# A segment's stored keys and queries fetched as one group of four loads, two of them into unused partitions of the value tiles

## The chip, the cores and the metric

The kernel runs on one core of a Trainium2 chip. The metric is the device time of one execution in microseconds, the median of three runs. The engines are named as in the profile: PE is TensorE (PEld its weight load), DVE is VectorE, ACT is ScalarE, POOL is GpSimd and SP is SyncE; L1130 is line 1130 of the kernel.

## The reference, cut to what matters

Four layers, A, B, A, B, each added to its input, on 2048 tokens of 640 features. Only the A layers matter here:

```python
for s in range(n_seg):                      # 64 segments of 32 tokens
    h = concat([mem, xs])                   # 8 memory rows + 32 tokens = 40
    q, k, v = h @ Wq, h @ Wk, h @ Wv        # 32 heads of 192
    p = softmax(where(mask, q @ k.T * scale, -1e9))
    o = (p @ v) @ Wo
    mem = o[:8]                             # the next segment needs these
    outs.append(o[8:])
```

The memory rows of one segment come out of the segment before, so the 64 segments of a layer form a chain.

## The kernel before, in words

**Stored tokens.** Of a segment's 32 tokens, 24 pass through the chain together with the 8 memory rows; the keys, queries and values of the last 8 tokens don't depend on the memory and are worked out ahead of the chain for all segments (`A_pre`) and kept in DRAM: `kqb_d[round, partition, segment, 192]` for keys and queries, `vb_d` for values. The output rows of these tokens ("tails") take a way of their own.

**Rounds.** The 32 heads are worked through in four rounds of eight heads, numbered here 0 to 3 in the order in which a segment takes them (even segments take the heads forwards, odd ones backwards: `rounds(s)`). For each round the chain projects queries, keys and values of the 32 live rows (`project`, L1154), ACT moves them out of PSUM (L1169), DVE transposes them into the tile `QK` (L1174), POOL copies the round's stored keys and queries next to them, in columns 64 to 79 of each block of 80 (`extra_kq`, L1130), PE forms the scores (`scores`, L1191), ACT the exponentials (L1273), and PE multiplies by the values (`attend`, L1204; L1217 for the tail rows). The values stand in one of two tiles `Vs[n % 2]`: partitions 0 to 63 come from the projection (`v_rows`, L1181 and L1183), partitions 64 to 79 from `vb_d` by a DMA (`extra_v`, L1134); matmuls read partitions 0 to 79, and partitions 80 to 127 are unused. At a segment's end the output projection (L1263) is finished, and DVE writes the new memory rows (L1453, L1455), on which the next segment's first query matmul waits.

**Order.** The scheduling in the chain is manual: each engine runs its instructions in the order in which the program lists them, and the queues of POOL and SP too, so that an instruction behind a waiting one waits as well. POOL issues nearly all the small DMAs. Its order in a segment before the change:

- Rounds 0 to 2, each: copies for the next round (`next_kq`, L1391, behind the scores of this round, since the copies overwrite what these read), a load of values (`tails_after`, L1405; in round 2 it comes behind the next scores, L1428), and one load of stored keys and queries, for three rounds later (`fetch_kq`, L1406), into one of two tiles `kqb`. In round 2 a store of tail rows (L1256) as well.
- Round 3: the value load for the next segment's round 0 (L1428), the copies for that round (L1429), the value load for its round 1 (L1435), one load of keys and queries (L1436), the rows of the segment after next (`load_rows`, L1101), and the tail loads (`load_tails`, L247), if there are any; then the stores of the finished rows (L1119, L1256).

**Tail loads.** The values of stored tokens for the later segments are worked out in the chain itself, a piece a segment. Their tokens are fetched once in eight segments: at the end of a segment `load_tails(s + 1)` (L1449) issues two loads, and in the next segment `turn_tails` (L1362) has DVE transpose them (L250), behind the value eviction of round 0 and ahead of the transposes of round 1's keys and queries. This happens for segments 7, 15, 23, 31, 39 and 47 of each chain, 24 loads in all.

**Start of a chain.** Two loads of stored keys and queries and two value loads are issued, the copies for the first round made, and a third load issued (L1323 on), while SP streams weights.

Of the kernel before, what the change touches and what calls it, by code (L numbers as in the profile page):

```python
# [8 lines left out]
P = 128  # L9
# [113 lines left out]
class Kernel:  # L123
# [934 lines left out]
    def A_chain(self, xn_dram, at_dram, li, load_slot, piece, late_wo, load_both, wo, low):  # L1058
        nc, tc, KC, NSEG = self.nc, self.tc, self.KC, self.NSEG
        scale = float(self.Dh) ** -0.5  # L1060
        NR = 4
        with tc.tile_pool(name=f"A{li}_ch", reuse_waits="tile", bufs=1) as sp, \
# [55 lines left out]
            def store_rows(s):  # L1118
                nc.gpsimd.dma_start(out=self.rows_d[32 * s:32 * s + 32, :].rearrange("t (q f) -> q t f", q=4), in_=orow)  # L1119

            def load_kqb(s, r):
                kqb = sp.tile([P, 192], BF16, name="kqb", tag="kqb", bufs=2)
                nc.gpsimd.dma_start(out=kqb[:], in_=self.kqb_d[r, :, s, :])  # L1123
                return kqb

            def extra_kq(kqb):
                for b in range(2):
                    h = slice(64 * b, 64 * b + 64)
                    o = QK[h].rearrange("p m (x c) j -> p (m x) c j", x=2)[:, :, b:b + 3, 64:80]
                    nc.gpsimd.tensor_copy(out=o, in_=kqb[h, :].rearrange("p (x c q) -> p x c q", c=3, q=16))  # L1130

            def extra_v(s, n):
                r = rounds(s)[n]
# [170 lines left out]
                    nc.scalar.activation(out=self.two_heads(vt), in_=ps[:, 0:384].rearrange("p (e f) -> p e f", e=2), func=ACT.Copy)  # L1304
                    self.store_values(nc.sync, vt, k, *unit)

            turns = [(s, r) for s in range(NSEG) for r in rounds(s)]

            def next_kq(s, n):

                at = NR * s + n + 1
                if at < len(turns):
                    extra_kq(kqs.pop(0))

            def fetch_kq(s, n):

                if s == 1:
                    self.copy_tails((2 * n, 2 * n + 1))
                at = NR * s + n + 3
                if at < len(turns):  # L1320
                    kqs.append(load_kqb(*turns[at]))

            kqs = [load_kqb(0, r) for r in rounds(0)[0:2]]  # L1323
            late_wo(0)
            extra_v(0, 0)
            extra_v(0, 1)
            extra_kq(kqs.pop(0))
            kqs.append(load_kqb(0, rounds(0)[2]))
            load_rows(1)
            for s in range(NSEG):  # L1330
                W = pop.tile([P, 512], F32, name="ps_w", tag="w")
                order = rounds(s)
                L = NR - 1

                def q_or_k(m, n, halves=False):
                    ps = psk if m == "K" else psq
                    project(hT, ps, m, n, s, range(KC))
                    return to_rows(ps, m, halves)

                def v_banks():  # L1340
                    return pop.tile([P, 512], F32, name="ps_v", tag="v")

                def tails_after(n):
                    if n + 2 < NR:
                        extra_v(s, n + 2)
                    elif s + 1 < NSEG:
                        extra_v(s + 1, n + 2 - NR)

                if s > 0:
                    keep_rows(W_done)  # L1350
                    rows = tail_rows(rct, spare_rows())
                    otb = turn_tail(rows)
                    store_rows(s - 1)
                    store_tail(otb, s - 1, rounds(s - 1)[L])
                turn_rows(q_or_k("Q", 0))
                turn_rows(q_or_k("K", 0))
                if s == 0:
                    late_wo(3, range(OWN // 2))
                pv = v_banks()
                project(hT, pv, "V", 0, s, range(KC))  # L1360
                v_rows(pv, 0, "sv")
                turn_tails(s)  # L1362
                OTs = []

                def turn(n, osc):
                    if n in (0, 2):
                        rows = (raw_of["K"][:, 0:384] if n else ots).rearrange("p (c j) -> p c j", j=64)
                        OTs.append([rows[:, 3 * G:3 * G + 3, :] for G in range(2)])
                        nc.vector.transpose(out=rows, in_=osc.rearrange("p (c j) -> p c j", j=64))
                        return  # L1370
                    if n == L:
                        OTs.append([KT[:, 3 * G:3 * G + 3, 0:64] for G in range(2)])
                    else:
                        OTs.append([vt[:, VH * G:VH * G + 192].rearrange("p (c j) -> p c j", j=64) for G in range(2)])
                    parts = osc if n == L else [osc[:, 192 * G:192 * G + 192] for G in range(2)]
                    for v, part in list(zip(OTs[n], parts))[::-1 if n == L else 1]:
                        nc.vector.transpose(out=v, in_=part.rearrange("p (c j) -> p c j", j=64))  # L1377

                outs = [(j, i) for j in range(L) for i in range(0, 12 if j else OWN, 2)]

                def output_steps(n):
                    for j, i in outs[0:n]:
                        wo_round(W, order[j], OTs[j], False, False, range(i, i + 2))
                    del outs[0:n]

                for n in range(L):
                    raw = q_or_k("Q", n + 1)
                    if n == 2:
                        otb = turn_tail(otr)
                    E = weigh()  # L1390
                    next_kq(s, n)  # L1391
                    turn_rows(raw)
                    if n == 1:
                        step = wo_round(W, order[0], OTs[0], True, False, range(OWN, 12))
                        if s == NSEG - 1:
                            load_both(order[L], True)
                            self.kept_tails = []
                            self.release(step, 12)
                            tails = self.kept_tails
                        else:  # L1400
                            load_both(order[L], False)
                    raw = q_or_k("K", n + 1, n + 1 == L)
                    O = attend(E, n)
                    if n != 2:
                        tails_after(n)  # L1405
                    fetch_kq(s, n)  # L1406
                    if n == 2:
                        store_tail(otb, s, order[1])
                    rc = weigh_rows(O)
                    if n == 1:  # L1410
                        rct = weigh_tail()
                    turn_rows(raw)
                    if n == L - 1:
                        output_steps(STEPS[0])
                    pv = v_banks()
                    project(hT, pv, "V", n + 1, s, range(KC))
                    if s == 0 and n == 1:
                        late_wo(1)
                        late_wo(2)
                    osc = raw_of["Q"][:, 0:384]  # L1420
                    for G in range(2):
                        scaled(osc[:, 192 * G:192 * G + 192], O, rc, G, "s")
                    turn(n, osc)
                    v_rows(pv, n + 1, "sv")
                    if n == 1:
                        otr = tail_rows(rct, raw_of["K"][:, 0:192])
                E = weigh(E)
                tails_after(2)  # L1428
                next_kq(s, L)  # L1429
                output_steps(STEPS[1])  # L1430
                if s + 1 < NSEG:
                    hT = new_hT()
                    hx_transpose(hT)
                O = attend(E, L)
                tails_after(L)  # L1435
                fetch_kq(s, L)  # L1436
                rc = weigh_rows(O)
                oscs = [raw_of["Q"][:, 192 * G:192 * G + 192] for G in range(2)]
                for G in (1, 0):
                    scaled(oscs[G], O, rc, G, "s")  # L1440
                keep_values()
                turn(L, oscs)
                output_steps(len(outs))
                if s == NSEG - 1:
                    self.spread_tails(0, tails[0], low, "vv")
                if s + 2 < NSEG:
                    load_rows(s + 2)
                wo_round(W, order[L], OTs[L], False, True, (*range(6, 12), *range(6)))
                load_tails(s + 1)  # L1449
                next_values(s)  # L1450
                if s + 1 < NSEG:
                    wt = raws[:, 0:640].bitcast(F32).rearrange("p (a b t) -> p a b t", a=2, b=KC)
                    nc.vector.transpose(out=wt, in_=W[:, 0:320].rearrange("p (a j b) -> p a b j", a=2, b=KC))  # L1453
                    for a in range(2):
                        nc.vector.tensor_tensor(out=hT[64 * a:64 * a + 64, :, 0:8], in0=wt[0:64, a, :, 0:8],  # L1455
                                                in1=wt[64:P, a, :, 0:8], op=ALU.add)
                rct = weigh_tail()
                W_done = W
# [92 lines left out]
```

## Time and profile before

| | |
|---|---|
| median of three runs | 3176.66 us (3176.52 to 3177.76) |
| profiled execution | 3169.9 us, span 3168.0 us |
| granted TensorE clock, mean | 0.992 |
| POOL copies of stored keys and queries, L1130 | 1024 of 341 ns |
| their loads, L1123 | 512 of 48 KB, 571 ns of POOL each, landing 4.3 us after issue (median) |
| value loads, L1134 | 512 of 24.2 KB, 504 ns, landing after 3.8 us |
| row loads, L1101, and row stores, L1119 | 126 and 128, 713 ns each |
| tail loads, L247 | 24 of 40 KB, 686 ns (median), landing after 5.2 us |

Durations of instructions and the sums in the text come from the one profiled execution, whose own time stands beside its span; the runs that give the median aren't profiled. A line of a wait list says which engine and line sat idle, until what was done, for how many us in total, how many times, and how long at most. A line of the instructions in order of time gives the start and the length in us, engine, line, operation, output and input with shapes, how many instructions are merged in it, and in brackets the idle time ahead of it with what ended it.

### The profile page before, as it was taken

Reading aid. Unit: us, or ns where it says so; the run is one execution under the profiler, and the core shown is the slowest. Engines: PE = TensorE matmul, PEld = TensorE weight load, DVE = VectorE, ACT = ScalarE, POOL = GpSimd, SP = SyncE. Lnnn points to the kernel's source line nnn. Section 1 sums busy time; section 2 is a strip of 40 time slices with the busy share of each in tenths; the row PEclk is TensorE's granted clock in tenths of the full one; section 3 lists DMA queues with packets and bytes.
Section 4 is the critical chain, followed back from the end, with each engine's and each line's share of the span. In section 5 each row is a group of like instructions: output and inputs, shape, how many; then the busy total and the mean of one; then the engine's idle time right before and its main releaser. Section 6 shows DMA issues by size and latency. Waiting matters only on the chain.

```text
span 3168.0 us, 141538 instructions
## 1 busy us (share of the span) xinstructions
PE 2993.8 (95%) x59586; PEld 1920.6 (61%) x59586; DVE 2184.4 (69%) x5426; ACT 1906.3 (60%) x4536; POOL 1392.8 (44%) x2872
## 2 busy tenths in 40 slices
PE   8789999999999999899999999999999999998999
PEld 7656666666666665555377566666666666665553
DVE  5467777777777777656644677777777777776565
ACT  3356666666666666646433566666666666666453
POOL 3255555555555555430122555555555555554300
PEclk9999999999999999999999999999999999999999
DMA  9977777877877877840268777777877777778300
GB/s 377 340 263 257 261 248 251 265 257 250 272 252 251 267 256 246 288 166 1 103 246 320 257 255 246 263 264 245 264 259 249 255 261 255 246 259 287 130 1 34
DMA packets 338873, 749.67 MB, mean 237 GB/s; under 512 B 68874, under 2 KB 115330, under 8 KB 335166
## 3 DMA queue, kind: packets, MB, share of 16 engines
q1 hardware_dynamic: 267998, 636.89, 58.3%
q0 software_dynamic: 69376, 100.10, 10.9%
q8 instruction: 469, 7.68, 1.0%
q10 hardware_dynamic: 864, 3.64, 0.3%
q14 instruction: 166, 1.36, 0.1%
HBM read 670.77 MB, written 78.01 MB: 236 GB/s over the span
## 4 chain that ended last, share of the span: by engine, by line
PE 76%; DVE 8%; DMA 6%; issue 5%; ACT 3%; POOL 2%; ACTq 0%; DVEq 0%; SPq 0%; POOLq 0%
PE ps_qk_k L1154 13%; PE ps_qk_q L1154 13%; PE ps_v L1154 12%; PE ps_w L1263 11%; PE ps_s L1191 6%; PE ps_pre L985 4%; PE ps_o L1204 3%; PE kv L1506 2%; DVE raws L1453 2%; ACT raws L1234 2%; DVE hT L1455 2%; PE ps_pq L517 2%; PE ps_t L1217 1%; PE ps_wo L466 1%; DVE QK L1377 1%
## 5 line engine op out<-in xcount | busy, mean ns | idle before, releaser
L1154 PEld LDWEIGHTS <-hT 128*32 128x32 bf16 x30720 | 787.1, 96 | 461.0 <-DVE hT L1455 78.7
L1174 DVE STREAM_TRANSPOSE QK<-raws 128x512 bf16<-128x512 bf16 (+1 forms) x1152 | 730.0, 642 | 219.3 <-ACT raws L1169 163.7
L1130 POOL COPY QK<-kqb 64x192 bf16<-64x192 bf16 x1024 | 349.5, 341 | 486.6 <-PE ps_s L1191 254.1
L1154 PE MATMUL ps_qk_q<-arena,hT 128*32 128x384 bf16 x10240 | 511.3, 327 | 41.4 <-DVE hT L1455 25.6
L1154 PE MATMUL ps_qk_k<-arena,hT 128*32 128x384 bf16 x10240 | 510.1, 328 | 3.0 <-ACT E L1273 1.4
L1169 ACT ACTIVATE raws<-ps_qk_k 128x512 bf16<-128x512 f32 (+1 forms) x640 | 313.5, 510 | 254.0 <-PE ps_qk_k L1154 243.5
L1234 ACT ACTIVATE raws<-ps_o,under 128x192 bf16<-128x192 f32 x1024 | 373.8, 420 | 121.9 <-DVE under L1228 102.5
L1154 PE MATMUL ps_v<-arena,hT 128*32 128x384 bf16 x8192 | 428.4, 326 | 4.0 <-issue 3.0
L1169 ACT ACTIVATE raws<-ps_qk_q 128x512 bf16<-128x512 f32 x512 | 305.7, 597 | 166.6 <-PE ps_qk_q L1154 153.1
L1134 POOL DMA_DIRECT2D Vp<-vb x512 | 257.9, 504 | 316.6 <-PE ps_t L1217 210.7
L1123 POOL DMA_DIRECT2D kqb<-kqb x512 | 292.4, 571 | 69.7 <-POOL QK L1130 59.4
L1191 PEld LDWEIGHTS <-QK 128*80 128x80 bf16 x4096 | 196.0, 121 | 184.9 <-issue 153.8
L1183 DVE CAST Vp<-ps_v 64x384 bf16<-64x384 f32 x512 | 286.3, 559 | 24.5 <-ACT Vp L1181 8.7
L1263 PE MATMUL ps_w<-arena,under 128*32 128x320 bf16 x6144 | 280.6, 300 | 9.5 <-DMA arena<-wo_rows 4.1
L1191 PE MATMUL ps_s<-QK 128*80 128x80 bf16 x4096 | 253.4, 209 | 21.8 <-POOL QK L1130 13.6
L1181 ACT ACTIVATE Vp<-ps_v 64x384 bf16<-64x384 f32 x512 | 246.4, 481 | 35.1 <-PE ps_v L1154 33.6
L1273 ACT ACTIVATE E<-ps_s 80x320 bf16<-80x320 f32 x512 | 217.7, 425 | 42.8 <-PE ps_t L1217 28.6
L985 PEld LDWEIGHTS <-arena 128*128 128x128 bf16 x1920 | 187.9, 98 | 31.0 <-issue 4.7
L1119 POOL DMA_DIRECT2D attn<-under x128 | 91.3, 713 | 262.0 <-DVE under L1115 223.5
L1112 ACT ACTIVATE raws<-ps_w 64x160 f32<-64x160 f32 x256 | 76.6, 299 | 201.1 <-DVE raws L1453 199.6
L1204 PE MATMUL ps_o<-Vp,E 80*32 80x193 bf16 x4096 | 180.3, 248 | 10.2 <-issue 5.7
L1263 PEld LDWEIGHTS <-under 128*32 128x32 bf16 x6144 | 147.2, 96 | 41.6 <-issue 9.8
(167 smaller groups left out, 4360.5 us busy)
## 6 DMA issues: line engine op xcount, KB each, us to landing
arena<-wo_rows SPq DMA_DIRECT2D x560, 320.0 KB, 4.8
arena<-in_A_Wq_dram SPq DMA_DIRECT2D x427, 384.0 KB, 4.5
arena<-in_A_Wk_dram SPq DMA_DIRECT2D x298, 384.0 KB, 5.6
arena<-in_A_Wv_dram SPq DMA_DIRECT2D x290, 384.0 KB, 5.9
kqb<-kqb POOLq DMA_DIRECT2D x512, 48.0 KB, 4.3
kqb<-arena POOLq DMA_DIRECT2D x14, 1536.0 KB, 9.7
Vp<-vb POOLq DMA_DIRECT2D x512, 24.2 KB, 3.8
otb<-otb POOLq DMA_DIRECT2D x256, 48.0 KB, 4.0
```

Source lines behind the costliest of these rows:

```text
L985: nc.tensor.matmul(ps[:, T * i:T * i + T], lhsT=w[b][:, P * c:P * c + P], rhs=xBT[:, b, :], start=(b == 0), stop=(b == KC - 1))
L1123: nc.gpsimd.dma_start(out=kqb[:], in_=self.kqb_d[r, :, s, :])
L1130: nc.gpsimd.tensor_copy(out=o, in_=kqb[h, :].rearrange("p (x c q) -> p x c q", c=3, q=16))
L1134: nc.gpsimd.dma_start(out=Vs[n % 2][64:80, :], in_=self.vb_d[s // 8, r].rearrange("g (t s) x f -> s (g t) (x f)", s=8)[s % 8])
L1154: last = nc.tensor.matmul(o, lhsT=hT[:, b, :], rhs=rhs, start=(i == 0), stop=(i == KC - 1), tile_position=(0, 32 * g), skip_group_check=True)
L1169: nc.scalar.activation(out=raw[:, c], in_=ps[:, c], func=ACT.Copy)
L1174: nc.vector.transpose(out=o, in_=i)
L1183: nc.vector.tensor_copy(out=o, in_=i)
L1191: nc.tensor.matmul(S[0:80, c0:c0 + 80], lhsT=KT[:, 4 * x + c, :], rhs=QT[:, 4 * x + c, :], start=(c % 2 == 0), stop=(c % 2 == 1), skip_gro ...
L1204: nc.tensor.matmul(O[G][32 * h:32 * h + 32, VH * G:VH * G + 193], lhsT=E[0:80, 80 * h + 32 * G:80 * h + 32 * G + 32], rhs=V[0:80, VH * h:V ...
L1234: nc.scalar.activation(out=out, in_=i, func=ACT.Copy, scale=rc[G])
L1263: step = nc.tensor.matmul(W[q:q + 32, 0:320], lhsT=OT[i // 6][:, i % 6 // 2, 32 * (i % 2):32 * (i % 2) + 32], rhs=rhs, start=(first and i ...
```

## The change

`load_kqb` takes the position of the round in its segment. The loads for positions 0 and 1 still go to a `kqb` tile of 128 partitions. Those for positions 2 and 3 go to partitions 96 to 127 of the value tiles, four pieces of 32 partitions side by side, 192 columns each; `extra_kq` then makes four copies of 32 partitions instead of two of 64, from partitions 96 to 127 to each quarter of `QK`. All four loads that a segment's copies will need next (its rounds 1, 2, 3 and the following segment's round 0) are issued as one group, in round 3 of the segment in front, behind the copies made there and ahead of the value load, the row load and the tail loads. The loads in rounds 0 to 2 and the one behind the value load of round 3 are gone. At the start of a chain one load is issued, and the group for the first segment behind the first copies.

```diff
-            def load_kqb(s, r):
+            def load_kqb(s, n):
+                rows = self.kqb_d[rounds(s)[n], :, s, :]
+                if n > 1:
+                    kqb = Vs[n % 2][96:P, 0:768].rearrange("p (g q) -> p g q", g=4)
+                    nc.gpsimd.dma_start(out=kqb, in_=rows.rearrange("(g p) q -> p g q", g=4))
+                    return [kqb[:, g, :] for g in range(4)]
                 kqb = sp.tile([P, 192], BF16, name="kqb", tag="kqb", bufs=2)
-                nc.gpsimd.dma_start(out=kqb[:], in_=self.kqb_d[r, :, s, :])
-                return kqb
+                nc.gpsimd.dma_start(out=kqb[:], in_=rows)
+                return [kqb[0:64, :], kqb[64:P, :]]
 
             def extra_kq(kqb):
-                for b in range(2):
-                    h = slice(64 * b, 64 * b + 64)
-                    o = QK[h].rearrange("p m (x c) j -> p (m x) c j", x=2)[:, :, b:b + 3, 64:80]
-                    nc.gpsimd.tensor_copy(out=o, in_=kqb[h, :].rearrange("p (x c q) -> p x c q", c=3, q=16))
+                step = P // len(kqb)
+                for i, rows in enumerate(kqb):
+                    o = QK[step * i:step * i + step].rearrange("p m (x c) j -> p (m x) c j", x=2)
+                    b = step * i // 64
+                    nc.gpsimd.tensor_copy(out=o[:, :, b:b + 3, 64:80], in_=rows.rearrange("p (x c q) -> p x c q", c=3, q=16))
...
-            def next_kq(s, n):
-
-                at = NR * s + n + 1
-                if at < len(turns):
+            def next_kq():
+                if kqs:
                     extra_kq(kqs.pop(0))
 
-            def fetch_kq(s, n):
-
-                if s == 1:
-                    self.copy_tails((2 * n, 2 * n + 1))
-                at = NR * s + n + 3
-                if at < len(turns):
-                    kqs.append(load_kqb(*turns[at]))
-
-            kqs = [load_kqb(0, r) for r in rounds(0)[0:2]]
+            def fetch_kqs(s):
+                kqs.extend(load_kqb(s, n) for n in range(1, NR))
+                if s + 1 < NSEG:
+                    kqs.append(load_kqb(s + 1, 0))
+
+            kqs = [load_kqb(0, 0)]
             late_wo(0)
             extra_v(0, 0)
             extra_v(0, 1)
-            extra_kq(kqs.pop(0))
-            kqs.append(load_kqb(0, rounds(0)[2]))
+            next_kq()
+            fetch_kqs(0)
             load_rows(1)
...
                     O = attend(E, n)
                     if n != 2:
                         tails_after(n)
-                    fetch_kq(s, n)
+                    if s == 1:
+                        self.copy_tails((2 * n, 2 * n + 1))
...
                 E = weigh(E)
                 tails_after(2)
-                next_kq(s, L)
+                next_kq()
+                if s + 1 < NSEG:
+                    fetch_kqs(s + 1)
                 output_steps(STEPS[1])
...
                 O = attend(E, L)
                 tails_after(L)
-                fetch_kq(s, L)
+                if s == 1:
+                    self.copy_tails((2 * L, 2 * L + 1))
```

More of the change, by code (lines that the diff above doesn't have):

```diff
@@ L1305, in keep_values @@
                     self.store_values(nc.sync, vt, k, *unit)
-            turns = [(s, r) for s in range(NSEG) for r in rounds(s)]
-            def next_kq(s, n):
-                at = NR * s + n + 1
-                if at < len(turns):
+            def next_kq():
+                if kqs:
                     extra_kq(kqs.pop(0))
-            def fetch_kq(s, n):
-                if s == 1:
-                    self.copy_tails((2 * n, 2 * n + 1))
-                at = NR * s + n + 3
-                if at < len(turns):
-                    kqs.append(load_kqb(*turns[at]))
-            kqs = [load_kqb(0, r) for r in rounds(0)[0:2]]
+            def fetch_kqs(s):
[3 more added lines that the diff above has]
+            kqs = [load_kqb(0, 0)]
             late_wo(0)
@@ L1428, in A_chain @@
                 tails_after(2)
-                next_kq(s, L)
+                next_kq()
+                if s + 1 < NSEG:
+                    fetch_kqs(s + 1)
                 output_steps(STEPS[1])
```

1 line of the change is left out of this document (removed).

## The prediction, made before the changed kernel was run

> **What bounds the kernel now.** I read the page's first part, then the waits, then a usual segment instruction by instruction, then the segments that start late.
>
> ```profile
> PE 2993.8 (95%) x59586; PEld 1920.6 (61%) x59586; DVE 2184.4 (69%) x5426; ACT 1906.3 (60%) x4536; POOL 1392.8 (44%) x2872
> ```
>
> TensorE is busy for 95% of the span, and nearly all of it lies in the 128 segments (64 in each of the two chains), which run one behind the other. Segments take 17.93 us at least and 18.3 us in the median (from one first query matmul to the next). So what counts is only what makes TensorE wait. GpSimd, where the change is made, is busy for 44%; 642 of its 1393 us are the copies (L1130, 349.5) and load issues (L1123, 292.4) that the change touches. The waits (who waited for whom: us in total, times, longest) tell whether it holds TensorE:
>
> ```profile
> PEld L1191 <- issue: 153.8, 470, 1.3
> POOL QK L1130 <- DMA kqb<-kqb: 129.4, 83, 5.0
> ...
> PEld L1191 <- POOL QK L1130: 30.1, 44, 13.8
> ```
>
> In the second line the copies at L1130 sat 129.4 us on stored keys and queries that had not landed. The third is what of it reached the scores: 30.1 us. But 13.8 of that is one wait, at the start of the first chain, and the first line says that a score's weight load has 153.8/470 = 0.33 us of idle time ahead of it anyhow. The other 43 waits are 16.3 us, less 43 x 0.33 = 14.1: **about 2 us** are truly lost. A usual segment shows why (start, us, engine, line):
>
> ```profile
> 615.62 0.50 PE L1191 MATMUL ps_s<-QK 128*80 128x80 bf16 x8
> ...
> 616.59 0.74 POOL L1130 COPY QK<-kqb 64x192 bf16<-64x192 bf16 x2 [1.15 <-DMA kqb<-kqb]
> ...
> 618.23 0.50 PE L1191 MATMUL ps_s<-QK 128*80 128x80 bf16 x8
> ```
>
> The copies for the last round waited for their DMA, ended at 617.33, and the scores that read them came 0.9 us later.
>
> **A place where GpSimd's order does reach TensorE.** In a usual segment the second round's scores start 3.205 us after the first's. Apart from the first segment of each chain, 10 segments are 0.2 to 1.7 us late with them, all of them segments in which turn_tails moves a freshly loaded set of tail rows (12 do: 7, 15, ... 47 of each chain; the other two are on time). One of them:
>
> ```profile
> 286.64 0.49 POOL L1134 DMA_DIRECT2D Vp<-vb  x1
> ...
> 287.19 0.60 POOL L1123 DMA_DIRECT2D kqb<-kqb  x1
> ...
> 287.79 0.71 POOL L1101 DMA_DIRECT2D xr<-xn  x1
> ...
> 288.49 1.36 POOL L247 DMA_DIRECT2D under<-tails  x2
> ...
> 292.74 0.47 PE L1191 MATMUL ps_s<-QK 128*80 128x80 bf16 x8
> ...
> 293.58 0.38 DVE L250 STREAM_TRANSPOSE tT<-under 128x160 bf16<-128x160 bf16 x1 [0.39 <-DMA under<-tails]
> ...
> 294.56 0.37 DVE L250 STREAM_TRANSPOSE tT<-under 128x160 bf16<-128x160 bf16 x1 [0.61 <-DMA under<-tails]
> ...
> 294.85 0.67 DVE L1174 STREAM_TRANSPOSE QK<-raws 128x512 bf16<-128x512 bf16 x1
> ...
> 295.64 0.69 DVE L1174 STREAM_TRANSPOSE QK<-raws 128x512 bf16<-128x512 bf16 x1
> ...
> 296.48 0.47 PE L1191 MATMUL ps_s<-QK 128*80 128x80 bf16 x8 [0.46 <-DVE QK L1174]
> ```
>
> The two tail loads are the last of four kinds of DMA that GpSimd issues back to back; VectorE waits for them at L250, and its next two transposes are the keys and queries of round 1. Measured from the first round's scores, the twelve second L250 transposes end at 2.19, 1.89, 1.20, 1.98, 2.51, 2.58 (first chain) and 3.15, 2.07, 3.40, 1.93, 1.39, 2.66 us, and the next scores start at 3.73, 3.44, 3.21, 3.53, 4.06, 4.13, 4.69, 3.61, 4.94, 3.47, 3.20, 4.21: always 1.54 us behind, once that is past 3.205. The wait isn't made up later: the three latest have segments of 20.40, 19.74 and 19.98 us.
>
> **The change, part by part.** Against the profiled execution's own 3169.9 us (span 3168.0).
>
> 1. *The group of four loads.* It is issued behind the copies of the last round, in front of the Vp load, the xr load and the tail loads; the single kqb load that stood there goes. The two loads into a kqb tile cost 0.571 us of issue each (L1123's mean). The two into 32 partitions by four pieces have no row: from below the same 0.571, from above the 0.713 of L1101 and L1119, which also split rows in four; I take 0.713, the nearer form. The group is 2 x 0.571 + 2 x 0.713 = 2.57 us, less 0.57: the Vp load of the next segment's second round, xr and the tails start **2.0 us later** (1.7 at the low end, and then 20 in place of this part's 23.3). The Vp load starts 11 us before its use and lands in 3.8, xr a segment ahead; the row stores behind them wait for VectorE 1.6 to 2.0 us already, and nothing waits for them within the segment; the next copies have 1.5 us of idle time ahead of them. All this costs nothing, and 0.5 us a segment if that idle time were gone. The tail loads have no cover: with the same time to landing, ten of the twelve segments get 2.0 us more, and the two that are on time use up 0.46 and 0.27 of slack: 20.0 + 1.54 + 1.73 = **+23.3 us**.
>
> 2. *Their landing.* They land 4.0 to 6.1 us after issue (median 5.2). The DMA engines are 0.20 busy in the last 2.4 us of a segment and 0.99 from 4 us on, as the windows show (the fields behind POOL's: granted clock, DMA share, GB/s), so a later issue meets more weights:
>
> ```profile
> 604.70:608.70 4.00, 3.97 (x92) 2.55 (x96) 3.16 (x7) 2.74 (x6) 1.37 (x3) 1.00 0.76 211
> 608.70:612.70 4.00, 4.00 (x108) 2.74 (x104) 3.21 (x6) 2.93 (x8) 2.38 (x6) 1.00 0.99 351
> ...
> 620.70:623.15 2.45, 2.11 (x42) 1.03 (x34) 1.56 (x5) 1.06 (x4) 1.56 (x3) 1.00 0.20 43
> ```
>
> The two of the twelve that were issued latest took 6.0 us, the other ten 5.2. Bounds: no change, and 1.5 us more (the 7 us that loads take in the crowded first segment); I take half of the seen 0.8: 12 x 0.4 = **+5 us** (0 to +18).
>
> 3. *Copies of 32 partitions.* Rounds 2 and 3 get four copies instead of two. GpSimd's copies of 128x120, 64x192 and 128x320 take 283, 341 and 453 ns: a line in the elements of a partition (173 + 0.87 each), the partitions don't count, and L691's copies from the lower to the upper half fit it (64 elements, 231). So 2 x 0.35 us more each time. Behind the first scores shown above, four copies end at 616.15 + 1.40 = 617.55, ahead of 618.23; in round 1 the slack is 2.5 us. **0**, hidden by the projection of keys and values. From above: if a 32-partition copy cost twice as much they would end at 618.95, 0.75 us late in 126 segments, +95 us.
>
> 4. *The waits at L1130 that go.* Round 1's load now has 6 us, the rest 9 to 18, against a landing of 4.3 (2.3 for the loads that are issued at this place now; longest 6.9 in the running chain): **-2 us**, the excess worked out above; at most the full -16. What is late next is the projection in front of the scores.
>
> 5. *Chain starts.* The first segment's second load is issued behind the first copies (near 151.4) and lands 5 us later, as the load at 151.59 does now, so its scores go from 156.03 to about 157.1; TensorE idles 1.7 us for Wq a little later and takes most of that back. In the second chain the load issued at 1727.7 lands at 1734.4, with scores due at 1731.1: 3.7 us late at most, and 2.9 us of waiting for Wq behind them. **+1 us** for both (0 to +6).
>
> 6. *DMA traffic.* Three loads of four leave the crowded middle, 16 packets of 3 KB and 0.126 us each on 16 engines: 0.4 of 12 us. TensorE's idle time put down to "issue", the matmuls alone, is 12 us in the first chain. All of both chains gone is -24, an equal loss +24; 3% of it is -1: **0**.
>
> The sum is 23.3 + 5 - 2 + 1 = +27 us: 3197 for the profiled execution. The runs' median, 3176.7, is 6.8 above that execution, so 3203.7 for the changed kernel.
>
> [...]
>
> **Rivals.**
> - *The freed middle pays* (not slower). If the crowded DMA stretch is what delays TensorE's instructions and weights, taking three loads out of it gives up to the full -16 of part 4 and -24 of part 6: 3203.7 - 14 - 24 = 3166. For it: matmuls do idle on "issue", and the stretch is at 0.99. Against it: the relief is 3%; 6.7 of the 12 us are at L1263, mostly at the segment's end, where the share is 0.2 to 0.65; and no weight is waited for in usual segments to speak of. It decides once the two parts bring 27 us more than I gave them.
> - *Tail loads lose less*: a group issued at 0.571 each and landing no later gives 20 - 2 + 1 = +19, 3196; in my range.
> - *Dear copies*: part 3's upper bound, 3300. The 231 ns of L691 speak against it.
> - *The value tile is tied up*: if the matmuls that read the tile's lower partitions had to wait for the load into the upper ones, each segment's last round would stand some 5 us, +600 in all. Against it: in 196 of 512 rounds the eviction into partitions 0 to 63 starts before the rows 64 to 79 of the same tile have landed.
>
> **How the numbers follow.** Forecast 0.78 (the smaller loss among it), the freed middle 0.12, dear copies 0.03, the tied tile 0.02, something else on the slow side 0.05. The forecast's own terms run from 20 - 16 + 0 + 0 = +4 to 23 + 18 + 6 - 2 = +45, and some 3 us either way of part 6: 3178 to 3225. The range is that, to 3226; it leaves out most of the freed middle and the last three cases, some 2 in 10. 0.2%, 6.4 us, is about what a measurement of this kernel can tell from no change. Faster by more: 0.04, a third of the freed middle. Within: 0.12, half of it and 0.06 from the forecast's low end. Slower: 0.84.
>
> **What would show it.** Waits: L1130 on kqb near zero; VectorE at L250 on the tails up from 12.9 us in 17 waits to some 40 in 24. Tail loads issued about 1.5 us before the first scores, not 3.5; in those twelve segments the second scores 5.2 to 7 us behind the first, the others unchanged at 3.2. L1130's group twice as large, at 0.34 us. I am wrong if the twelve segments aren't later, or if the other 116 change by more than 0.05 us on average.

## The result, and the profile after

The changed kernel takes **3226.99 us** (median of 4 runs, 3225.75 to 3230.58), the kernel before 3176.59 beside it: a ratio of **1.0165**, interval 1.0146 to 1.0184, so 50 us slower. The forecast was 27 us slower, at most 49. Interval here and below means a 95% interval. The profiled execution took 3225.75 us with a span of 3224.0, 56.0 more than the span of before (3168.0); the sums below are made against these 56. (They are more than 50 because the profiled execution of before lies 6.7 us below the median of its runs, that of the changed kernel 1.2 us.)

Of the changed kernel, first the line of busy times:

```profile
PE 3013.4 (93%) x59552; PEld 1930.2 (60%) x59586; DVE 2187.6 (68%) x5426; ACT 1910.3 (59%) x4536; POOL 1566.9 (49%) x3384
```

GpSimd's 174 us more are its copies of keys and queries, off the path: 1536 instead of 1024, half as many again and not twice as many, as the prediction had it, since only two of the four rounds got more. But TensorE, whose work is the same, is 19.6 us *busier*. The granted clock is 0.984 on the mean of this execution and was 0.992 before: this is the first sign of what the forecast lacks. Then the waits (who waited for whom: us in total, times, longest):

```profile
DVE tT L250 <- DMA under<-tails: 43.9, 24, 3.4
...
PE ps_s L1197 <- DVE QK L1180: 37.5, 13, 3.8
...
POOL QK L1136 <- DMA kqb<-kqb: 11.7, 3, 5.1
```

The first is the sign that the forecast had named, some 40 us in 24 waits on tail rows: 43.9 us (12.9 before). The second is what of it reaches TensorE: the scores of round 1 wait for keys and queries that VectorE transposes behind the tails. The third shows that the copies no longer wait for their loads (129.4 us before): what the change set out to remove is removed. Now one of the twelve segments with new tail rows (start, us, engine, line):

```profile
897.16 0.36 DVE L250 STREAM_TRANSPOSE tT<-under 128x160 bf16<-128x160 bf16 x1 [2.77 <-DMA under<-tails]
...
898.73 0.36 DVE L250 STREAM_TRANSPOSE tT<-under 128x160 bf16<-128x160 bf16 x1 [1.21 <-DMA under<-tails]
...
900.64 0.73 PE L1197 MATMUL ps_s<-QK 128*80 128x80 bf16 x8 [3.41 <-DVE QK L1180]
...
901.38 1.26 PE L1269 MATMUL ps_w<-arena,under 128*32 128x320 bf16 x16
...
902.42 1.78 PE L1160 MATMUL ps_qk_k<-arena,hT 128*32 128x384 bf16 x20
```

TensorE stands still for 3.41 us, and what follows is slow: eight scores in 0.73 us instead of 0.50, twenty projection matmuls in 1.78 instead of 0.99. The windows of the same stretch give the reason (behind POOL's field: granted clock, DMA share, GB/s):

```profile
895.90:897.20 1.30, 1.30 (x36) 0.64 (x24) 0.04 (x1) 0.10 (x1) 0.94 (x2) 1.00 1.02 300
897.20:900.60 3.40, 0.03 (x4) 0.00 (x0) 2.05 (x5) 0.62 (x2) 1.49 (x4) 1.00 1.04 384
900.60:902.40 1.80, 1.75 (x24) 1.22 (x28) 1.49 (x3) 1.40 (x4) 0.84 (x3) 0.51 0.65 216
902.40:904.30 1.90, 1.90 (x40) 1.06 (x36) 0.36 (x1) 0.04 (x1) 0.53 (x2) 0.57 0.03 11
```

The granted clock is 0.50 for 3.41 us (900.63 to 904.04) right behind the wait, and 1.00 again behind that. In the kernel before, the same segment has the full clock behind its wait of 0.8 us:

```profile
884.70:886.70 2.00, 1.73 (x44) 1.26 (x48) 1.75 (x3) 1.34 (x4) 0.68 (x2) 1.00 1.03 377
```

The half clock comes in ten of the twelve segments and in no segment of this kind before, where the waits were 1.7 us at most. In the ten, round 2's scores start 5.2 to 6.3 us behind round 1's; in the two with a full clock, 4.09.

Measured between the first score matmuls of the rounds, the 56.0 us divide so:

| where | us |
|---|---|
| 12 segments with new tail rows, from round 0's scores to round 1's (3.85 to 6.38 us on average) | +30.3 |
| the same, from round 1's to round 2's (4.22 to 5.22): the half clock | +12.0 |
| the same, the rest | -3.1 |
| first segment of each chain | +5.2 |
| the other 114 segments: rounds 1 and 2 +0.08 and +0.09 each, last stage -0.10 | +8.9 |
| outside, by difference | +2.7 |

The smaller rows differ from execution to execution. In the traces of three more kernels below, whose 114 other segments run the same program, these cost 11.0, 13.7 and 16.3 us. And the first segments, 66.1 us long together here and 61.0 before, take 58.6 to 62.4 us in the five traces of kernels with the chain start of before and 62.1 to 66.1 in the eight with the changed start: some 3 us more on average.

### The profile page after: what moved, and what is told of

The parts are those of the page before. It is cut to its first block, busy times and chain, and to the rows that moved or that the text cites. A ratio compares the mean times of both kernels' runs of the same rounds, so it can differ in the third digit from the quotient of the medians.

```text
span 3224.0 us, 142134 instructions
## 1 busy us (share of the span) xinstructions
PE 3013.4 (93%) x59552; PEld 1930.2 (60%) x59586; DVE 2187.6 (68%) x5426; ACT 1910.3 (59%) x4536; POOL 1566.9 (49%) x3384
## 4 chain that ended last, share of the span: by engine, by line
PE 75%; DVE 8%; DMA 7%; issue 4%; ACT 3%; POOL 2%; SPq 0%; DVEq 0%; POOLq 0%; ACTq 0%
PE ps_qk_k L1160 13%; PE ps_qk_q L1160 12%; PE ps_v L1160 12%; PE ps_w L1269 10%; PE ps_s L1197 6%; PE ps_pre L985 4%; PE ps_o L1210 3%; DMA under<-tails 2%; PE kv L1509 2%; DVE raws L1456 2%; PE ps_wo L466 2%; ACT raws L1240 2%; PE ps_pq L517 1%; DVE hT L1458 1%; PE ps_t L1223 1%
## 5 line engine op out<-in xcount | busy, mean ns | idle before, releaser
L1136 POOL COPY QK<-Vp 32x192 bf16<-32x192 bf16 x1024 | 351.6, 343 | 371.0 <-issue 281.5
L1160 PE MATMUL ps_qk_k<-arena,hT 128*32 128x384 bf16 x10240 | 521.6, 332 | 10.7 <-issue 9.8
L1189 DVE CAST Vp<-ps_v 64x384 bf16<-64x384 f32 x512 | 286.2, 559 | 29.1 <-ACT Vp L1187 13.6
L1136 POOL COPY QK<-kqb 64x192 bf16<-64x192 bf16 x512 | 174.9, 342 | 204.2 <-PE ps_s L1197 171.7
L985 PEld LDWEIGHTS <-arena 128*128 128x128 bf16 x1920 | 187.1, 98 | 30.3 <-issue 5.4
L1230 DVE RECIPROCAL under<-ps_o 128x2 f32<-128x2 f32 x384 | 65.5, 171 | 160.9 <-PE ps_o L1210 154.7
```

What stands on the lines that cost most here:

```text
L985: nc.tensor.matmul(ps[:, T * i:T * i + T], lhsT=w[b][:, P * c:P * c + P], rhs=xBT[:, b, :], start=(b == 0), stop=(b == KC - 1))
L1136: nc.gpsimd.tensor_copy(out=o[:, :, b:b + 3, 64:80], in_=rows.rearrange("p (x c q) -> p x c q", c=3, q=16))
L1160: last = nc.tensor.matmul(o, lhsT=hT[:, b, :], rhs=rhs, start=(i == 0), stop=(i == KC - 1), tile_position=(0, 32 * g), skip_group_check=True)
L1189: nc.vector.tensor_copy(out=o, in_=i)
```

## The experiments

Ratios are to runs of the kernel before on the same chip, whose median was 3168.7 us beside the two kernels with the tail loads first, the one with late tails and the one with extra matmuls; 3169.1 beside those with the dummy loads, the order of the twelve undone, four copies, and the first two loads together; 3173.3 beside the two with the group in a quieter place and the repeat; and 3180.6 beside the one with a quarter of the bytes. So differences between kernels of different groups are read from ratios and traces, not from times. Of each edit the main lines are shown.

**Tail loads first.** In the changed kernel (and, second, in the kernel before) the tail loads are issued behind the copies of the last round:

```diff
                 next_kq()
+                load_tails(s + 1)
                 if s + 1 < NSEG:
                     fetch_kqs(s + 1)
 ...
-                load_tails(s + 1)
                 next_values(s)
```

> The changed kernel, with the two tail loads issued ahead of the group of four instead of 1.5 us behind where they were. Theory (late tails cost it all but some 14 us: the twelve segments lost 30 us in front of round 1's scores and 12 us more behind them): both losses go, and so does the 7.8 us that the kernel before lost at the same place; what stays is 5 us at the two chain starts and 9 us spread over the other segments: 3177 - 8 + 14 = 3183. Rival (the group's other effects, its traffic and the copies of 32 partitions, carry the loss): it stays above 3210. Second rival (the 14 us are chance): 3169.

> The kernel before, with the two tail loads moved to the same place, behind the copies of the last round. Theory: the twelve segments start round 1's scores 3.205 us behind round 0's, 0.65 us earlier on average: 3176.6 - 7.8 = 3169. Rival: the loads now lie in the crowded stretch of DMA traffic and hold up weights or row stores there, and nothing is gained: 3177 or more.

Measured: 3198.6 us, ratio **1.0084** (1.0067 to 1.0100, 27 us), and 3168.1, **0.9998** (0.9985 to 1.0011). In both traces no tail is waited for. Both theories missed; of the second kernel the rival was right that nothing is gained. The changed kernel without its tail waits is still 27 us slower, not 6; and the kernel before gains nothing from the 7.8 us. So there is a second cost. In the traces it is TensorE standing still for 0.25 to 2.4 us at scattered places, with "issue" as the reason, the profile's word for idle time in which an engine waits for nothing that it shows. One from the repeat of the first kernel (below):

```profile
753.22 0.50 PE L1197 MATMUL ps_s<-QK 128*80 128x80 bf16 x8
755.73 1.00 PE L1160 MATMUL ps_qk_k<-arena,hT 128*32 128x384 bf16 x20 [2.02 <-issue]
```

The DMA records show a fetch of 16 KB of instructions from 753.09 to 754.20, 1.5 us ahead of the restart. It is so each time: in the 14 profiles here there are 610 such stalls of more than 0.25 us from the second segment's first scores to the last segment's last in each chain, and every one ends 1.20 to 1.67 us behind the end of an instruction fetch, where fetches come some 6 us apart. They sum to 23.4 us before, 27.8 in the changed kernel, 29.2 in the kernel before with the tails first, and **47.3** in the changed one with the tails first. In the twelve segments alone (and the two others at their place in the count of eight) they are 2.9 us before, 7.5 and 7.6 in these two, and 1.5 in the changed kernel: there a wait for tails seems to stand in for a stall. That is 6 of the 20 us by which the stalls of the two changed kernels differ. The other 13 lie in segments whose program is the same in both and in which no tails are waited for; those 114 segments cost 31 us over the kernel before with the tails first and 9 in the changed kernel. Why, no run here shows.

**Tails late, alone.** Three GpSimd copies ahead of the tail loads of the kernel before:

```diff
                 if new_set(s):
+                    for c in (768, 768, 176):
+                        nc.gpsimd.tensor_copy(out=Vs[0][96:P, 0:c], in_=Vs[1][96:P, 0:c])
                     for half in range(2):
```

> The kernel before, with three GpSimd copies of 2.0 us together (an estimate from its line of 173 ns and 0.87 ns an element) in front of the tail loads of the twelve segments, between partitions that nothing reads; no group, no new copies of keys and queries. Theory (late tails alone): issue 2.0 us later, landing takes 6.0 instead of 5.3 us as in the changed kernel, 12 x 2.6 = 31 us, and 12 to 15 us more by the halved clock that follows an idle time of 2.5 to 3.4 us: 3176.6 + 45 = 3222 (3215 to 3226). Rival (only the wait itself counts, and the rest of the changed kernel's loss comes from its group): 3176.6 + 24 to 28 = 3203.

Measured: 3194.7, ratio 1.0073 (1.0051 to 1.0095, 23 us). A flawed experiment: the copies delayed TensorE by themselves, so that the tail loads were issued only 1.3 us later against the scores and landed 0.6 us later, and only one of the twelve waits brought the half clock. Its trace shows the collision:

```profile
1030.68 2.10 POOL L1290 COPY Vp<-Vp 32x768 bf16<-32x768 bf16 x3
...
1031.03 1.41 DVE L1457 TENSOR_TENSOR hT<-raws 64x40 bf16<-64x40 f32 x2
...
1032.49 1.00 PE L1154 MATMUL ps_qk_q<-arena,hT 128*32 128x384 bf16 x20 [1.14 <-DVE hT L1457]
```

VectorE's two additions take 0.43 us in every other segment; beside these copies they took 0.76 to 1.72, in 11 of the 12 segments, and the next segment waits for them. The delay had to be made without an engine's work.

**The same with loads.** Three loads into partitions that nothing reads, ahead of the tail loads of the twelve segments:

```diff
                 if new_set(s):
+                    for n, h in ((0, slice(80, 96)), (0, slice(96, P)), (1, slice(96, P))):
+                        rows = self.kqb_d[n, 0:4 * (h.stop - h.start), s, :]
+                        nc.gpsimd.dma_start(out=Vs[n][h, 0:768].rearrange("p (g q) -> p g q", g=4),
+                                            in_=rows.rearrange("(g p) q -> p g q", g=4))
                     for half in range(2):
```

> The kernel before, with three more loads of stored keys and queries into partitions that nothing reads (48, 48 and 24 KB), issued in front of the tail loads of the twelve segments only: the group's delay without its copies, and without a change in the other 116 segments. Theory: tail loads issued 1.7 us later and landing 6 us after issue, 25 to 31 us in front of round 1's scores, and 10 to 13 us by the halved clock: 35 to 44 us over the kernel before. Rival (only the delay itself, at an unchanged landing time and a full clock): 20 us over it.

Measured: 3222.1, ratio **1.0155** (1.0127 to 1.0182, 49 us), near that of the whole change, with no group, no new copies and 116 unchanged segments. Its waits:

```profile
DVE tT L250 <- DMA under<-tails: 48.7, 22, 4.9
...
PE ps_s L1191 <- DVE QK L1174: 42.3, 13, 5.4
```

Tail loads issued 1.7 us later landed 3.0 us later. In front of round 1's scores that is 35.2 us, behind them 15.9, with the half clock behind ten of the twelve waits; the rival's 20 us are out. The runs are above the theory's 35 to 44 us, whose upper end the interval (40 to 58) still holds; the trace, of the fastest of the four runs, has 39 us over that of before, with 9 us less in the other segments.

**The clock alone.** Extra matmuls where TensorE would idle:

```diff
+                flat = hT.rearrange("p j b -> p (j b)")
+                for _ in range(fill):
+                    nc.tensor.matmul(S[:, 320:480], lhsT=flat[:, 0:P], rhs=flat, start=True, stop=True,
+                                     skip_group_check=True)
 ...
-                    E = weigh()
+                    E = weigh(fill=32 if n == 1 and new_set(s) else 0)
```

> The changed kernel, with 32 extra matmuls (128 x 160, into columns of the scores' bank that nothing reads, some 2.1 us at full clock) in front of round 1's scores in the twelve segments, where TensorE idles 2.5 to 3.8 us. Theory (the idle time halves the granted clock for 3.4 us in ten of the twelve, and that is the 12 us behind round 1's scores): the clock stays at 1.00, round 2's scores come 4.1 us behind round 1's instead of 5.2, round 1's as late as before: 3227 - 13 = 3214. Rival (late weights or instruction fetches behind the wait): no change, 3227, with the clock at 1.00 but the gap still at 5.2 us.

Measured: 3215.8, ratio 1.0147 (1.0123 to 1.0170), that is 47 us over the kernel before, where the changed kernel is 50 over it. The two intervals overlap, and the runs alone can't tell a gain of 13 us from none. The trace can, at the place in question. The same segment as above; the extra matmuls take 2.39 us, where the 2.1 of the expectation was the author's estimate:

```profile
898.64 2.39 PE L1196 MATMUL ps_s<-hT 128*128 128x160 bf16 x32
901.33 0.47 PE L1201 MATMUL ps_s<-QK 128*80 128x80 bf16 x8 [0.30 <-DVE QK L1180]
902.07 0.73 PE L1273 MATMUL ps_w<-arena,under 128*32 128x320 bf16 x16 [0.27 <-DVE under L1372]
902.62 0.99 PE L1160 MATMUL ps_qk_k<-arena,hT 128*32 128x384 bf16 x20
```

Round 1's scores are as late as ever (6.33 us behind round 0's on average, 6.38 without the filling), but the matmuls behind them have their usual times again, the clock is 1.00 in all twelve, and round 2's scores follow after 4.05 us instead of 5.22: 14 us at this place, from work that is thrown away. So the slow matmuls behind the waits are the half clock's doing. The span is 3209.7, 14.3 less than the changed kernel's, but of one execution each, and the four runs of this kernel lie 12 us apart: that the whole kernel gains as much isn't shown.

**Only the order of the twelve undone.**

```diff
-                    fetch_kqs(s + 1)
+                    fetch_kqs(s + 1, (1,) if new_set(s + 1) else (1, 2, 3, 4))
 ...
                 load_tails(s + 1)
+                if new_set(s + 1):
+                    fetch_kqs(s + 1, (2, 3, 4))
```

> The changed kernel; in front of the twelve segments only, the last three of the four loads are issued behind the tail loads, which so keep the place they had in the kernel before. All else as changed. Theory (the tail loads' delay and the halved clock behind it cost 42 us): that comes back, and 9 to 14 us over the kernel before stay. Rival (as the kernel with the tails first, where 27 us stayed although no tail was waited for): the group's traffic costs more than the trace of the changed kernel shows, and 25 us or more over the kernel before stay.

Measured: ratio 1.0057 (1.0038 to 1.0076, 18 us): some two thirds of the 50 us come back by this order alone. That is between the two expectations; by its trace the other 114 segments cost 14 us.

**Copies of 32 partitions alone**, in the kernel before:

```diff
-                    extra_kq(kqs.pop(0))
+                    extra_kq(kqs.pop(0), 32 if (n + 1) % NR > 1 else 64)
```

> The kernel before, with the keys and queries of rounds 2 and 3 copied by four copies of 32 partitions instead of two of 64. Theory (343 ns each and hidden by the projection of keys and values): 0, within 4 us of the kernel before. Rival (GpSimd's longer stretches hold up VectorE or the next issues): 10 us or more over it.

Measured: 3195.2, ratio 1.0078 (1.0051 to 1.0105, 25 us). The expectation missed. The wait of the scores for the copies, 30.1 us in 44 times before, is now

```profile
PEld L1191 <- POOL QK L1130: 59.4, 122, 11.9
```

In 57 of 128 last rounds the scores stop behind the first of their eight matmuls for the copies, some 23 us more than before at that place, and the tail loads go out 0.4 us later, another 6. A copy takes 343 ns, as forecast. But here the loads still land late: in 53 of the 57 the copies start 0.13 us behind the landing of their load. The slack is used up by waiting for it, and two copies more show. In the changed kernel the loads have landed and this stop occurs twice. So the earlier loads of the change pay for its costlier copies.

**The first two loads of a chain together again:**

```diff
-            kqs = [load_kqb(0, 0)]
+            kqs = [load_kqb(0, 0), load_kqb(0, 1)]
 ...
-                kqs.extend(load_kqb(s, n) for n in range(1, NR))
+                kqs.extend(load_kqb(s, n) for n in range(1 if s else 2, NR))
```

> The changed kernel, with the first two loads of a chain issued together as before, and the group of the first segment one load shorter. Theory: the first segments' four rounds of scores take 15.2 us again instead of 18.6 and 16.6 us, 5 us less: 3222. Rival (the first segment waits for weights in any case): no change, 3227.

Measured: 3226.7, ratio 1.0184 (1.0158 to 1.0210). No gain; in the trace the rounds of the first segments take 17.5 and 15.9 us, 1.8 less together. Such differences come without a change of the start, too: with the start of before these rounds take 15.2 and 15.1 us in the kernel before, but 18.7 and 15.4 in the one with four copies. Most of the 5 us is then scatter of single executions.

**The group in a quieter place.** Three of the four loads some 2.5 us earlier, and, second, the tails first besides:

```diff
                         store_tail(otb, s, order[1])
+                        if s + 1 < NSEG:
+                            fetch_kqs(s + 1, (1, 2, 3))
 ...
-                    fetch_kqs(s + 1)
+                    fetch_kqs(s + 1, (4,))
```

> The changed kernel, with three loads of the group (rounds 1 to 3 of the next segment) issued in the third round, behind its row store, some 2.5 us earlier than in the changed kernel, where the weight loads run out; the fourth stays alone behind the copies of the last round, as the one load of the kernel before. Theory (what stays of the loss besides the late tail loads is the group's traffic, at the end of the segment where the next segment's weights start: their loads land 0.7 us later and the crowd lasts on into rounds 1 and 2): tail loads as in the kernel before, weights land as in it, stalls of TensorE behind instruction fetches as in it: within 8 us of the kernel before, and better than the one with three loads behind the tails (12 to 24 us over it). Rival (the group costs this wherever it lies, by the copies or by the middle it leaves): 12 to 24 us over the kernel before.

> The same, with the two tail loads ahead of the fourth load. Theory: no tail wait is left, 7.8 us less than the kernel before at that place, and nothing lost elsewhere: 5 to 15 us faster than the kernel before. Rival (as when the kernel before had its tails moved: the 7.8 us come back as stalls behind instruction fetches): the same time as the kernel before.

Measured: 1.0054 (1.0031 to 1.0078, 17 us) and **1.0023** (1.0011 to 1.0035, 7 us). The first is what its rival said, the second slower than both of its expectations. With the tails first, the quiet place is worth 18 us (1.0080 or 1.0084 to 1.0023); its stalls behind fetches are 30.9 us. In the first of the two, the tail loads are still issued 0.55 us later than before against the scores and cost 15 us. Neither is faster than the kernel before; no version tried here is, with its work complete.

**Chance or program, and traffic or order.** The first kernel again, and then with a quarter of the bytes in each load of the group:

```diff
+            two = [sp.tile([P, 192], BF16, name=f"kqb{i}") for i in range(2)]
 ...
-                    nc.gpsimd.dma_start(out=kqb, in_=rows.rearrange("(g p) q -> p g q", g=4))
+                    some = 1 if s else 4
+                    nc.gpsimd.dma_start(out=kqb[:, 0:some, :], in_=rows[0:32 * some].rearrange("(g p) q -> p g q", g=some))
 ...
-                kqb = sp.tile([P, 192], BF16, name="kqb", tag="kqb", bufs=2)
-                nc.gpsimd.dma_start(out=kqb[:], in_=rows)
+                kqb = two[n]
+                some = 32 if s else P
+                nc.gpsimd.dma_start(out=kqb[0:some], in_=rows[0:some])
```

> The changed kernel with the tail loads first once more, unchanged, to see whether its 47 us of stalls behind instruction fetches (changed kernel 28, kernel before 23) belong to the program or to one loading of it. Theory (they belong to the traffic that the program makes): 45 us again and 27 us over the kernel before. Rival (chance of one loading): 25 to 30 us of such stalls, and 6 to 10 us over the kernel before.

> The changed kernel with the tail loads first, its group at the same place with the same four issues and the same copies, but from the second segment of a chain on each of the four loads brings only the first 32 of the 128 rows (three quarters of the stored keys and queries are left out, 36 of 48 KB a load). Theory (the 27 us that this kernel keeps over the one before, with no tail waited for, are its traffic at the segment's end): weights issued between 4.5 us ahead of and 3.2 us behind the first scores land in 5.2 us again instead of 5.9, stalls behind instruction fetches fall from 47 and 50 to 30 us or less, and the time is within 8 us of the kernel before. Rival (the copies of 32 partitions, or the issues themselves): 47 us of stalls and 27 us over it stay.

Measured: 1.0080 (1.0051 to 1.0109) with 50.4 us of stalls: they belong to the program. With a quarter of the bytes, same issues and copies: **0.9950** (0.9929 to 0.9972), 16 us *faster* than the kernel before, where the theory had it within 8; stalls 27.2 us. It leaves work out, and also moves fewer bytes than the kernel before. With the issues and copies unchanged, what the group costs is what its loads move (the bytes, and the packets with them); that the place matters too, the quieter place has shown. The effect on the weights, by the median landing of one kind of them (calls, KB, us to landing), in the kernel before, in the changed one, in the one with the tails first and in the one with a quarter of the bytes:

```profile
arena<-in_A_Wq_dram SPq DMA_DIRECT2D x427, 384.0 KB, 4.5
```

```profile
arena<-in_A_Wq_dram SPq DMA_DIRECT2D x427, 384.0 KB, 5.5
```

```profile
arena<-in_A_Wq_dram SPq DMA_DIRECT2D x427, 384.0 KB, 5.6
```

```profile
arena<-in_A_Wq_dram SPq DMA_DIRECT2D x427, 384.0 KB, 5.1
```

By the DMA records of segments away from the twelve, in the 1.5 to 3 us ahead of the first scores the weights' queue has 0.43 of the DMA engines before and 0.23 in the changed kernel, GpSimd's queue 0.13 and 0.30. The weights make up for it at 3 to 10 us, where their mean share rises from 0.89 to 0.95; there the stalls grow from 9.8 to 23.1 us, and behind it they fall from 13.6 to 4.7. That a fetch is later because it queues behind those weights is not shown: the records don't tell when a fetch was asked for. And the kernel with a quarter of the bytes speaks against so simple an account. Its weights issued between 4.5 us ahead of and 3.2 us behind the first scores land in 5.5 us (median), not in the 5.2 that the theory named (5.0 before, 5.9 with the tails first), and their share at 3 to 10 us is 0.94, as in the one with the tails first (0.95), yet the stalls there, outside the twelve segments and their two like, are 14 us against 35.

## Why the prediction was wrong

The direction and the first mechanism were right, the size was not: +50 for +27.

1. **The group in front of the tail loads, and their landing (steps 1 and 2): right.** 28.3 us forecast, 30.3 measured, in the twelve segments that were named. The parts were off against each other: issue 1.5 us later instead of 2.0, landing of the second load 1.0 us slower instead of 0.4. (Of the three segment lengths given as those of the latest, 20.40 us belongs to one that is 0.85 us late; the third latest has 19.25. All are above the median of 18.3, so the reading stands.)
2. **The step that failed: the wait was priced at its own length.** "The wait isn't made up later" was as far as the text went. TensorE stood still for 2.5 to 3.8 us in the twelve segments, and in ten of them it was slow afterwards as well, at a granted clock of 0.50 for 3.41 us (6.83 in one): +12.0 us, absent from the sum and from every rival. The trace of the changed kernel shows it, the dummy loads bring it about without the change, and the extra matmuls take it away at its place. The rows were there. The trace of before has the half clock behind its long idle stretches, at the chain starts (one of 2.92 us in the second chain's first segment, for instance), and none behind idle times up to 1.7 us; adding 2 us to 1.7 left the range in which it had been seen to cost nothing.
3. **Copies (step 3): 0, right here**, but for a reason that step 4 owned. Taken alone they cost 25 us, since their cover is the slack that only an early load leaves.
4. **Waits that go (step 4)**: they went, 129.4 to 11.7 us, and as forecast TensorE got next to nothing for it.
5. **Chain starts (step 5)**: +5.2 for +1, inside its bounds of 0 to 6; some 3 on the average of the traces, the rest scatter.
6. **DMA traffic (step 6): 0 was wrong, the second term that failed.** The text looked at the middle that three loads leave and not at the place they go to. It had quoted the DMA share of 0.20 in the last stretch of a segment, and did not ask what three loads more do there; but the group's loads land some 3 us after their issue, where the next segment's weights begin. The 114 other segments lost 8.9 us (0.08 each, beyond the 0.05 that the text had set as its own test), 11 to 16 in three more traces, and 31 in the kernel with the tails first. That it comes from what the loads move, the quarter loads show for the kernel with the tails first; how it makes the stalls, and why they are so many more there, stays open.

The rivals fared so: the tied value tile and the dear copies did not occur in this kernel; the freed middle fell short, since the stalls that the late rounds lost (9 us) the early ones gained (13 us); and the tail loads lost more, not less. That two loads of the group go into 32 high partitions did not show in their landing: these land in 3.0 us, those into 128 partitions in 3.2 (medians).

## What to carry to other kernels

Before adding a few us to a wait of the engine that bounds the kernel, look how long its idle time becomes, not only how much longer. Here waits of TensorE of up to 1.7 us cost their own length, and of those of 2.5 to 3.8 us ten in twelve put its next 3.4 us at half the clock, so that 30 us of delay cost 12 more. A DMA queue's quiet stretch is judged by when a load lands and what else starts then, not by the share at its issue. And take a change apart in the kernel before as well as in the changed one: here an earlier load hid dearer copies, and the kernel without its tail waits showed 47 us of stalls where 28 had been.

## What the runs showed of the hardware

**The clock.** In each profile nine in ten changes of the granted clock, or more, lie within 0.03 us of a grid of 3.413 us. Between two borders of the grid lies a window. Behind the first segments of the chains of all fourteen profiles, each of the 37 windows at full clock in which TensorE idled for 0.57 of the window (1.95 us) or more was followed by one at half the clock. Of 18 windows idle for 0.47 to 0.57, three were followed by one as well (0.48, 0.51 and 0.565) and 15 were not (up to 0.566); below 0.47 none was. So the border isn't sharp by this measure. It is the idle time in a window that goes with it, not the length of a wait: two waits of 3.13 and 3.16 us cost nothing more, since a window's border cut them into 1.6 + 1.5 and 1.9 + 1.3 us, while a wait of 1.43 us with another of 0.30 in the same window was followed by the half clock.

**Instruction fetches.** Some 420 fetches of 16 KB on the instruction queue lie in the segments of each profile; behind 27 to 69 of them TensorE stood still, for 13 to 50 us in all, which is 0.4 to 1.6% of this kernel.

**GpSimd beside VectorE.** In the kernel with late tails, VectorE's two small additions beside copies of 768 bf16 elements on 32 partitions took 0.76 to 1.72 us in 11 of 12 segments, against 0.43 in every other one. Why, no run here shows.
